# Four value loads moved from SyncE's DMA queue to ScalarE's in a retention-plus-FFN kernel

## The chip, the cores and the metric

The kernel runs on one core of a Trainium2 chip. The metric is the device time of one execution in microseconds, as the median of several runs. A "span" is the length of one profiled execution; it is about 2 us shorter than the time of the same run (196.0 against 198.11 us for the kernel before).

## The reference

Four sequences of 768 tokens with 8 heads of width 64 go through a decaying linear attention; the result, 3072 tokens of width 512, goes through a multiplicative FFN:

```python
# attention, per batch and head
state = gamma * state + outer(k[t], v[t])
y[t] = scale * (q[t] @ state)
# FFN on x = y of all heads side by side
out = ((x @ w1) * (x @ w2)) @ w3 @ w_out
```

All inputs and the output are float32. The kernel computes in fp16 with float32 accumulation, 24 chunks of 128 tokens.

## The kernel before

It first folds W3 and W_out into one matrix (TensorE transposes blocks of W3 and multiplies them with W_out), and the first chunks' attention is threaded into the end of that. All loads are issued by SyncE, in this order, at the very start of the program text:

```python
for i in range(4):
    w3c_st.append(load_w3_columns(i))
    wo_st.append(load_wo(i))
w3_st = {f: load_rows(moe_w3, f) for f in range(4, 8)}
load_chunk(0)                       # q of chunks 0 and 1, k and v of chunk 0
load_chunk(1)                       # k and v of chunk 1
w1_st = [load_rows(moe_w1, d) for d in range(4)]
w2_st = [load_rows(moe_w2, d) for d in range(4)]
for n in range(2, 6):
    load_chunk(n)
```

Each of these is 256 KB (k, v) or 512 KB (everything else). Nothing on SyncE has to wait for arithmetic here except W1 and W2, which reuse staging buffers.

The stretch into which the change reaches (cuts marked). `cast_w3` is a ScalarE cast of a W3 block to fp16, `w3_transpose` its transpose on TensorE, `w3_mm` the product with W_out with a copy of the result on ScalarE; `casts` is GpSimd's cast of q and k and its product of v with the decay factors:

```python
cast_w3(4, w3_st[4])
cast_w3(5, w3_st[5])
w3_mm_columns(3, acc)     # its last result is copied by ScalarE
w3_transpose(4)
w3_transpose(5)
cast_w3(6, w3_st[6])
w3_mm(4)
w3_transpose(6)
cast_w3(7, w3_st[7])
casts(0)
casts(1)
w3_mm(5)
# ... transposes, scores and kv of chunks 0 and 1, w3_mm(6), w3_mm(7) ...
cast_w(W1, w1_st, 1, False)
cast_w(W1, w1_st, 2, False)
cast_w(W1, w1_st, 3, True)      # True: on VectorE
cast_w(W2, w2_st, 0, True)
cast_w(W2, w2_st, 1, True)
```

Each engine has its own list of instructions, and the framework that builds the program adds the semaphores, counters that an instruction can wait for. In this program all hardware-queue transfers share eight completion semaphores, DMAHW0 to DMAHW7. (What is said here of the semaphores' names was read in the built programs. The traces don't name them; they show when an issue starts and when a transfer lands.)

## Time and profile before

| | |
|---|---|
| time | 198.95 us (198.35 to 199.02, 3 runs); 198.99 with a fourth run beside the changed kernel |
| span | 196.0 us |
| TensorE busy | 185.4 us, 95% |
| ScalarE busy | 97.1 us, 50% |
| transfers | 40.15 MB, the 16 engines nearly always busy for the first 150 us |

The page gives busy times and the chain of work that ended last. A line of a timeline is: start in us, duration in us, engine (SPq and ACTq are the sequencers of SyncE and ScalarE issuing transfers), source line, operation, what is written and read, count; in brackets the idle time before it and what ended it. The lines themselves stand in the prediction below.

### The profile page before, as it was taken

The numbers are of one execution on the slowest core, as the hardware profiler recorded it, in microseconds if no ns is written. First come the engines' busy times: TensorE is split into PE (matmuls) and PEld (weight loads), VectorE is DVE, ScalarE is ACT, GpSimd is POOL, SyncE is SP. The second block draws the span as 40 slices with busy tenths as digits, with TensorE's granted clock in tenths as the row PEclk, the third lists the DMA queues.
The fourth block names the chain that finished last, engine by engine and source line by source line (L and its number), as shares of the span: only waits on it lengthen the run. The fifth ranks groups of instructions, "written<-read, shape, count | busy, mean of one in ns | idle before, by whom it ended". The sixth has DMA issues, their size and how long they took to land.

```text
span 196.0 us, 4658 instructions
## 1 busy us (share of the span) xinstructions
PE 185.4 (95%) x1773; PEld 139.9 (71%) x1773; DVE 114.7 (59%) x215; ACT 97.1 (50%) x188; POOL 79.6 (41%) x137
## 2 busy tenths in 40 slices
PE   6798996999997999999999999999999999999992
PEld 2334665757995879778877887788778877887750
DVE  3226368757875767558555676575657665753310
ACT  6378547425443544546445454554455545534331
POOL 7200351166959636484423543854236432200000
PEclk9999999999999999999999999999999999999999
DMA  6999999989999999999999999979999630111112
GB/s 204 372 388 387 221 329 412 327 181 247 292 200 244 177 236 225 211 227 214 192 185 234 153 220 194 240 200 193 201 242 198 150 96 17 59 54 54 54 48 116
DMA packets 87446, 40.15 MB, mean 205 GB/s; under 512 B 67968, under 2 KB 82304, under 8 KB 87424
## 3 DMA queue, kind: packets, MB, share of 16 engines
q1 hardware_dynamic: 87424, 39.86, 91.0%
q8 instruction: 14, 0.23, 0.6%
q14 instruction: 8, 0.07, 0.2%
HBM read 29.36 MB, written 6.29 MB: 182 GB/s over the span
## 4 chain that ended last, share of the span: by engine, by line
PE 84%; DMA 6%; SPq 2%; DVE 2%; ACT 2%; POOL 1%; issue 1%; ACTq 0%; DVEq 0%; POOLq 0%
PE psF L427 39%; PE psO L453 21%; DMA stg<-in_moe_w_dram 6%; PE psA L361 5%; PE psW L254 4%; PE psY L399 3%; PE psY L400 3%; SPq L62 2%; PE psF L601 2%; PE psY L402 2%; PE psK L382 2%; PE psT L348 1%; PE psW L229 1%; DVE xt L407 1%; PE psYf L601 1%
## 5 line engine op out<-in xcount | busy, mean ns | idle before, releaser
L427 PE MATMUL psF<-xt,w 128*128 128x256 f16 (+1 forms) x768 | 87.1, 264 | 0.0
L427 PEld LDWEIGHTS <-w 128*128 128x128 f16 x768 | 68.1, 98 | 6.7
L437 ACT COPY pa<-psF 128x256 f32<-128x256 f32 x88 | 32.6, 372 | 35.7 <-PE psF L427 35.2
L443 DVE TENSOR_TENSOR ht<-pa,psF 128x256 f16<-128x256 f32 x88 | 36.7, 417 | 22.7 <-PE psF L427 10.6
L453 PE MATMUL psO<-w3o,ht 128*128 128x512 f16 x192 | 45.4, 379 | 0.2 <-DVE ht L620 0.2
L364 DVE TENSOR_TENSOR am<-psA,keep 128x512 f16<-128x512 f32 x48 | 30.9, 685 | 23.8 <-PE psA L361 23.8
L391 POOL TENSOR_TENSOR t<-s,GS 128x512 f16<-128x512 f32 x16 | 20.7, 1296 | 47.1 <-DVE s L390 38.7
L280 POOL TENSOR_TENSOR vp<-v,VS 128x256 f16<-128x256 f32 x48 | 28.5, 615 | 11.7 <-PE psY L402 5.7
L453 PEld LDWEIGHTS <-ht 128*128 128x128 f16 x192 | 18.5, 98 | 18.4 <-DVE ht L620 1.0
L458 ACT ACTIVATE osb<-psO 128x512 f32<-128x512 f32 x24 | 14.3, 597 | 34.2 <-PE psO L453 34.2
L270 POOL CAST q<-q 128x1024 f16<-128x1024 f32 x12 | 12.4, 1037 | 22.3 <-DMA q<-in_q_dram 22.1
L407 DVE TENSOR_TENSOR xt<-psY,YS 128x512 f16<-128x512 f32 x24 | 17.7, 736 | 5.4 <-PE psY L402 4.3
L276 POOL CAST k<-k 128x512 f16<-128x512 f32 x24 | 14.7, 611 | 7.7 <-PE psK L382 7.0
L399 PE MATMUL psY<-am,vp 128*128 128x128 f16 x96 | 16.7, 219 | 1.0 <-DVE am L364 0.9
L400 PE MATMUL psY<-am,vp 128*128 128x128 f16 x96 | 16.7, 219 | 0.0
L361 PEld LDWEIGHTS <-kp 128*128 128x128 f16 x192 | 12.6, 98 | 5.4 <-ACT kp L194 0.7
L390 DVE TENSOR_TENSOR s<-psK,t 128x512 f32<-128x512 f32 x16 | 11.0, 690 | 3.3 <-PE psK L382 3.0
L212 DVE COPY w3t<-psW 128x1024 f16<-128x1024 f16 x8 | 5.5, 690 | 11.9 <-PE psW L220 8.6
L342 ACT COPY kp<-kT 64x512 f16<-64x512 f16 x16 | 9.9, 618 | 1.9 <-DMA kT<-k 1.5
L400 PEld LDWEIGHTS <-vp 128*128 128x128 f16 x96 | 9.4, 98 | 1.5 <-issue 1.2
L194 ACT CAST w3h<-stg 128x1024 f16<-128x1024 f32 x8 | 8.3, 1044 | 4.1 <-DMA stg<-in_moe_w_dram 4.1
L402 PE MATMUL psY<-qTd,t 128*128 128x128 f16 x56 | 10.1, 219 | 0.0
(66 smaller groups left out, 170.6 us busy)
## 6 DMA issues: line engine op xcount, KB each, us to landing
stg<-in_moe_w_dram SPq DMA_DIRECT2D x16, 512.0 KB, 8.1
q<-in_q_dram SPq DMA_DIRECT2D x12, 512.0 KB, 5.0
k<-in_k_dram SPq DMA_DIRECT2D x24, 256.0 KB, 5.4
v<-in_v_dram SPq DMA_DIRECT2D x24, 256.0 KB, 5.3
out_dram<-osb SPq DMA_DIRECT2D x24, 256.0 KB, 2.4
stg<-in_moe_w_out_dram SPq DMA_DIRECT2D x4, 512.0 KB, 8.2
kT<-k SPq DMA_TRANSPOSE x16, 4.5
qTd<-q SPq DMA_TRANSPOSE x8, 4.3
```

What stands on the lines that cost most here:

```text
L276: nc.gpsimd.tensor_copy(k16[:, :], k32[:, :])
L280: nc.gpsimd.tensor_tensor(vp[:, :, r, r * 64 : r * 64 + 64], v32[:, :].rearrange("j (p s e) -> j p s e", s=2, e=64)[:, :, r, :], VS[:, :]. ...
L361: nc.tensor.matmul(ps[:, i, r, :], lhsT=kp[:, p, r, :], rhs=queries(n, p), start=True, stop=True)
L364: nc.vector.tensor_tensor(am[:, half * 2 : half * 2 + 2, :, :].rearrange("j p s i -> j (p s) i"), ps[:, :, :, :].rearrange("j p s i -> j ( ...
L391: nc.gpsimd.tensor_tensor(t16[:, :, :], s32[:, :, :], GS[:, :, :], MULT)
L399: nc.tensor.matmul(ps[:, p, :], lhsT=vp[:, p, 0, :], rhs=am[:, p, 0, :], start=True, stop=False)
L400: nc.tensor.matmul(ps[:, p, :], lhsT=vp[:, p, 1, :], rhs=am[:, p, 1, :], start=False, stop=(c == 0))
L407: nc.vector.tensor_tensor(XT[n // 2][:, :, n % 2 * C : (n % 2 + 1) * C].rearrange("p a (i t) -> p a t i", t=2), ps[:, :, :].rearrange(orde ...
L427: nc.tensor.matmul(ps[:, i * w : (i + 1) * w], lhsT=W[d][:, (f + i) * 128 : (f + i + 1) * 128], rhs=XT[self.tok0 // TB][:, d, c0 : c0 + w] ...
L437: nc.scalar.copy(self.pa[f][:, :], ps[:, :])
L443: nc.vector.tensor_tensor(self.HT[:, f : f + TB // self.width, :].rearrange("p f n -> p (f n)"), self.pa.pop(f)[:, :], ps[:, :], MULT,)
L453: nc.tensor.matmul(psO[:, :], lhsT=self.HT[:, f, tb * 128 : (tb + 1) * 128], rhs=W3O[f][:, :], start=(f == 0), stop=(f == 7),)
```

## The change

The intent: only q and k of the first chunks are urgent for TensorE's transposes; the values come later. If v of chunks 0 to 3 goes through ScalarE's own queue, issued when it is about to be needed, then W1, W2 and the next q and k move up in SyncE's queue.

```diff
+    def load_v(n):
+        chunk_in[n].append(load_kv(nc.scalar, "v", v, n))
 ...
         for nm, src in (("k", k), ("v", v)):
-            t = ld.tile([128, 512], FP, tag=nm + "32", name=nm + "32")
-            dma_in(...)
-            tiles.append(t)
+            if nm == "v" and n < 4:
+                continue
+            tiles.append(load_kv(nc.sync, nm, src, n))
 ...
     cast_w3(4, w3_st[4])
     cast_w3(5, w3_st[5])
+    load_v(0)
+    load_v(1)
     w3_mm_columns(3, acc)
 ...
     cast_w(W1, w1_st, 2, False)
+    load_v(2)
+    load_v(3)
     cast_w(W1, w1_st, 3, True)
```

(`load_kv` is the old body of the loop with the issuing engine as a parameter; cuts are marked with "...".)

More of the change, by code (lines that the diff above doesn't have):

```diff
@@ L65, with load_kv @@
     q_in = {}
+    def load_kv(eng, nm, src, n):
+        b, c = divmod(n, NCH)
+        t = ld.tile([128, 512], FP, tag=nm + "32", name=nm + "32")
+        eng.dma_start(
+            t[:, :].rearrange("p (h d) -> p h d", d=D),
+            src[b, :, c * C : (c + 1) * C, :].rearrange("h i d -> i h d"),
+        )
+        return t
+    def load_v(n):
+        chunk_in[n].append(load_kv(nc.scalar, "v", v, n))
     def load_chunk(n):
@@ L80, in load_chunk @@
         for nm, src in (("k", k), ("v", v)):
-            t = ld.tile([128, 512], FP, tag=nm + "32", name=nm + "32")
-            dma_in(
-                t[:, :].rearrange("p (h d) -> p h d", d=D),
-                src[b, :, c * C : (c + 1) * C, :].rearrange("h i d -> i h d"),
-            )
-            tiles.append(t)
+            if nm == "v" and n < 4:
+                continue
+            tiles.append(load_kv(nc.sync, nm, src, n))
         chunk_in[n] = tiles
```

## The prediction

> **What bounds the kernel now.** I began with the page: where each engine is busy, and the chain that ended last.
>
> ```profile
> PE 185.4 (95%) x1773; PEld 139.9 (71%) x1773; DVE 114.7 (59%) x215; ACT 97.1 (50%) x188; POOL 79.6 (41%) x137
> ...
> PE 84%; DMA 6%; SPq 2%; DVE 2%; ACT 2%; POOL 1%; issue 1%; ACTq 0%; DVEq 0%; POOLq 0%
> ```
>
> TensorE is busy for 185.4 of 196.0 us and carries 84% of the chain, so at most 10.6 us can be won. Then the waits of TensorE over the whole span say who owns those 10.6 us (columns: who waited, for whom, us in total, times, longest):
>
> ```profile
> PE psW L220 <- ACT w3h L194: 1.7, 4, 0.5
> PE psZ L534 <- DVE vp L133: 1.5, 1, 1.5
> PE psY L402 <- POOL t L391: 1.0, 1, 1.0
> PE psY L399 <- DVE am L364: 0.9, 1, 0.9
> PE psF L601 <- DVE xt L407: 0.6, 1, 0.6
> ```
>
> Only the first (W3 weights arriving, before 18 us) and the third (GpSimd late, at 59 to 60 us) have a transfer behind them. The change can't touch the first: all W3 loads are issued ahead of any value load.
>
> Next, ScalarE and TensorE in order of time around the place where the new issues stand. ScalarE (start, duration, what):
>
> ```profile
> 17.85 1.05 ACT L194 CAST w3h<-stg 128x1024 f16<-128x1024 f32 x1 [0.25 <-DMA stg<-in_moe_w_dram]
> 18.80 0.58 ACT L194 CAST w3o<-psWy 128x512 f16<-128x512 f32 x1
> 19.28 1.05 ACT L194 CAST w3h<-stg 128x1024 f16<-128x1024 f32 x1
> ```
>
> TensorE:
>
> ```profile
> 18.95 0.62 PE L229 MATMUL psW<-ident,w3h 128*128 128x128 f16 x8 [0.17 <-ACT w3h L194]
> 19.62 1.90 PE L254 MATMUL psW<-wo,w3t 128*128 128x512 f16 x8
> 21.36 0.61 PE L229 MATMUL psW<-ident,w3h 128*128 128x128 f16 x8
> 21.80 1.89 PE L254 MATMUL psW<-wo,w3t 128*128 128x512 f16 x8
> ```
>
> The ScalarE cast of 19.28 makes the fp16 rows of W3 block 6, which TensorE transposes at 21.36. It ends at 20.33, one microsecond early. In the windows view TensorE is busy for 10.00 of the 10 us from 20 to 30: what delays ScalarE by more than 1 us here delays the whole kernel.
>
> Last, the loads. SyncE's issues in order of time, and how long the issue of chunk 2's queries (at 28.26 us) took to land:
>
> ```profile
> 16.44 3.68 SPq L62 DMA_DIRECT2D v<-in_v_dram  x1
> 20.16 1.61 SPq L62 DMA_DIRECT2D k<-in_k_dram  x1
> 21.82 1.17 SPq L62 DMA_DIRECT2D v<-in_v_dram  x1
> 23.11 5.10 SPq L62 DMA_DIRECT2D stg<-in_moe_w_dram  x8
> 28.26 0.45 SPq L62 DMA_DIRECT2D q<-in_q_dram  x1
> ```
> ```profile
> DMA to landing us min/median/max: 11.9/11.9/11.9
> ```
>
> Adding the landing delay of each issue to its start gives a stream in strict order without a hole: k0 23.25, v0 24.6, k1 25.8, v1 26.8, the first W1 block 28.1, the last W2 block 37.0, chunk 2's q 40.1 (28.26 + 11.9), chunk 2's k 41.2. The transfer engines are the limit until about 50 us.
>
> **What the Trainium skill says.** "DMA: Bandwidth & Descriptors", section "Issuing engines are not separate DMA queues": transfers from different issuers run on the same 16 engines and interleave, and a second issuer saves only sequencer time. The trace of before has one issuing queue, so it can't show this; I take it as no gain in bandwidth. The same page, "Anatomy of one DMA": a transfer's semaphore wait is done by the issuing sequencer before dispatch. The trace agrees: chunk 2's q is issued at 28.26, just after the first W1 block has landed at 28.1, and the built program has it waiting for exactly that. "Perfetto Trace Analysis", section "DMA Instruction — HWDGE (DVE, Sync)": after that wait the sequencer locks the descriptor generator; not tested by one queue. "TensorE: Matmul & The Clock Gate", Part 1: after an idle window of about 3.4 us the array runs at half rate until it has been busy for such a window. The trace agrees: the first eight 128x512 matmuls take 3.60 us (450 ns each), five more from 6.42 us take 1.24 (248 ns).
>
> **The change part by part.** It takes four 256 KB loads off SyncE's stream and puts them on ScalarE: v0 and v1 after the cast of 17.85, v2 and v3 after the cast of W1 block 2.
>
> *The hidden part is a semaphore.* In the built programs every transfer takes the next of eight semaphores in program order and first waits until that semaphore's previous user has landed. The program text still issues the loads of chunks 2 to 5 at the top, before v0. In the changed program:
>
> ```
> SP   q, chunks 2 and 3  waits DMAHW7 >= 32, adds 16    (third user of DMAHW7)
> SP   k, chunk 2         waits DMAHW0 >= 48, adds 16
> ACT  v, chunk 0         waits DMAHW7 >= 48
> ACT  v, chunk 1         waits DMAHW0 >= 64
> ```
>
> So v0 can't be issued before chunk 2's q has landed, nor v1 before chunk 2's k. ScalarE meets these at about 19 us, and executes in order: behind them stand the copy of 18.80 and the cast of 19.28 that TensorE needs.
>
> *When does it go on?* Removing v0 and v1 from the stream advances all behind them by their own time, (24.6 - 23.25) + (26.8 - 25.8) = 2.35 us. So q of chunk 2 lands at 40.1 - 2.35 = 37.75 and k of chunk 2 at 38.85. v0 is issued from 37.75. An issue of k or v beside a full queue cost SyncE 1.0 to 4.3 us, and 1.0 at the least; ScalarE's own queue is empty, but the generator may be held by SyncE. I allow 1.7 us from k's landing to the end of the second issue (an estimate: 0.7 to issue, 1.0 for SyncE's turn): 40.6. Then the w3o copy holds ScalarE for 0.48 (18.80 to 19.28), the cast takes 1.05, and a handover 0.1: TensorE transposes at 42.2 instead of 21.36. **Delay: 20.9 us**, all of it on the path.
>
> *Cold restart.* TensorE has then idled for 20 us. At the start of before it took from 1.53 to about 6.4 us to reach full rate, some 4.4 us of them busy; half of that is lost: **+2.2 us**.
>
> *What comes back.* After the stall all first loads have landed. The wait of 1.0 us at 59 to 60 goes back to GpSimd's cast of chunk 6's q, which waited 1.44 us for its transfer behind a backlog; that backlog is gone: **-1.0 us**. W1 and W2 2.35 us earlier are worth nothing, as ScalarE is stopped.
>
> *v2 and v3.* Their semaphores are those of chunk 3's k and chunk 4's q, long landed by then. ScalarE idles 3.05 us just behind them (32.96 to 36.01 in before), so two issues of about 1 us cost nothing. Landing of v0: about 5 us after issue (4.6 to 5.7 in before beside a full queue), at about 43.5; its product is needed by the matmuls that stood at 26.82, now at about 48. Hidden.
>
> Sum: 198.95 + 20.9 + 2.2 - 1.0 = 221.05; I say **221**.
>
> **Rivals.**
> (a) *Only issue time.* If ScalarE didn't stop at the semaphore (or the wait were met at 19 us), two issues of 1.0 to 3.9 us (seen on SyncE) would stand before the cast, of which 1.0 is slack: +1 to +6 us, 200 to 205. Against it: the values 48 and 64 can't be reached before those loads land, which the trace puts near 40 us.
> (b) *The intended gain.* W1, W2, and the later q and k come 2.35 us earlier; with the only transfer-bound wait of TensorE after 20 us being 1.0, the gain would be at most 1 us: 198, within 2%. For it: the stream really is the bound of the loads until 50 us. Against: the semaphore again, and that TensorE waits for nothing of it.
> (c) *A longer stop.* The descriptor generator is shared, SyncE's issues hold it for 1 to 4 us each, and v0's packets alternate with those of chunk 2's k, so that k lands later and both issues take longer: up to 4 us more, 225. If v0 then landed later than 48 us, kv of chunk 0 would wait as well.
>
> **Range and chances.** The two landing times come from a stream in order and are good to about 1 us; the issues through a contended generator are uncertain by -1 to +3, the cold restart by 1 each way, the part that comes back by 1. I take 217 to 225 as the range. Rivals (a) and (b) need the wait to be absent from hardware though it stands in the program: 3% together, of which 2% within 2% and 1% faster.
>
> **What would show it.** ScalarE's timeline: a hole of about 20 us from 19 us on, ended by a transfer, with the two value issues on its queue near 38 and 39 to 40 us. TensorE: idle from about 21.4 to 42 before a transpose of W3, its releaser the w3h cast. Landing of chunk 2's q near 37.75. The first matmuls after the hole at about twice their duration start to start. From 60 us (before) on, the same distances shifted by a constant 21 to 23 us. The prediction is wrong if ScalarE works on through 20 to 38 us, if q of chunk 2 lands much earlier than 37 (a shorter stall), or if the issues on ScalarE take many microseconds each.

## The result

218.88 us (217.63 to 219.49, 4 runs) against 198.99 us (198.35 to 199.60, 4 runs). The ratio is 1.099 (95% interval 1.093 to 1.105). A ratio here is the mean time of one kernel's runs over that of the other's runs of the same rounds, so it isn't quite the ratio of the medians quoted.

The page of the changed kernel: TensorE's busy time hardly changed, its share fell. The rows of digits are tenths of busy time in 40 slices of 5.44 us; PEclk is the TensorE clock that was granted.

```profile
PE 186.8 (86%) x1773; PEld 140.3 (64%) x1773; DVE 115.7 (53%) x215; ACT 97.1 (45%) x188; POOL 80.5 (37%) x137
...
PE   6788000497799999999999999999999999999993
...
ACT  6473000537407454455554455564455464453332
...
PEclk9999755589999999999999999999999999999999
```

TensorE and ScalarE both stand still in three slices (22 to 38 us), and the granted clock is 0.7 in the first of them, then 0.5 until about 45.4 us, and full after that (0.52 from 43.5 to 45.4 us, 1.00 from 45.4 to 49). The work is the same; it is done later.

ScalarE in order of time, where the new issues stand (the lines that answer to those of 17.85, 18.80 and 19.28 us in the kernel before):

```profile
17.70 1.05 ACT L203 CAST w3h<-stg 128x1024 f16<-128x1024 f32 x1 [0.23 <-DMA stg<-in_moe_w_dram]
38.22 1.46 ACTq L70 DMA_DIRECT2D v<-in_v_dram  x2
39.72 0.58 ACT L203 CAST w3o<-psWy 128x512 f16<-128x512 f32 x1 [20.98 <-DMA k<-in_k_dram]
40.20 1.05 ACT L203 CAST w3h<-stg 128x1024 f16<-128x1024 f32 x1
```

It is the hole that was predicted: 20.98 us, ended by the landing of a **k**, though what stands in the queue are loads of **v**. Which k, and which q before it? Chunk 2's, issued by SyncE at 27.2 and 28.0 us. The next fence has what the trace says of these two issues (duration in ns, first and last start, then the time from issue to landing):

```profile
L62 SPq DMA_DIRECT2D q<-in_q_dram x1: 705/705/705, 27.2 to 27.2; - x1
DMA to landing us min/median/max: 11.0/11.0/11.0
L70 SPq DMA_DIRECT2D k<-in_k_dram x1: 666/666/666, 28.0 to 28.0; - x1
DMA to landing us min/median/max: 11.3/11.3/11.3
```

27.2 + 11.0 = 38.2: v0 is issued at 38.22. 28.0 + 11.3 = 39.3: v1 is issued at 39.30. Neither value load needs anything of chunk 2; they share its semaphores.

TensorE in order of time, against the lines of 19.62, 21.36 and 21.80 us of before:

```profile
19.47 1.90 PE L263 MATMUL psW<-wo,w3t 128*128 128x512 f16 x8
41.30 1.04 PE L238 MATMUL psW<-ident,w3h 128*128 128x128 f16 x8 [19.93 <-ACT w3h L203]
42.13 3.47 PE L263 MATMUL psW<-wo,w3t 128*128 128x512 f16 x8
45.43 0.61 PE L238 MATMUL psW<-ident,w3h 128*128 128x128 f16 x8
```

The transpose of W3 block 6 waits for its cast until 41.30 us, and the eight transposes and eight matmuls take 45.43 - 41.30 = 4.13 us where they took 23.53 - 21.36 = 2.17 us.

With start times of the same work on TensorE in both traces, the loss can be followed as it grows:

| TensorE starts | before | after | later by |
|---|---|---|---|
| transpose of W3 block 6 | 21.36 | 41.30 | 19.94 |
| transpose of W3 block 7 | 23.53 | 45.43 | 21.90 |
| first product with W1 | 32.92 | 54.82 | 21.90 |
| first output product (psO) | 40.76 | 63.50 | 22.74 |
| scores of chunk 3 | 47.43 | 70.17 | 22.74 |
| a later output product (psO) | 61.38 | 82.92 | 21.54 |
| end of the span | 196.0 | 217.6 | 21.6 |

So: +19.94 stop, +1.96 slow restart, +0.84 of something else at about 59 us, -1.20 given back at about 81 us, and nothing after that. The profiled run was the slowest of the four, and the profiled run of before was faster than its median; the medians differ by 19.9 us. So the hundredths hold for this pair of profiles alone. The stop itself varies from run to run: in e4 and e6 below, which issue the same loads in the same order, TensorE's transpose started at 40.59 and 40.41 us instead of 41.30.

The +0.84 was not in the prediction. TensorE's waits over the whole changed span show it as a new line, the second here:

```profile
PE psW L238 <- ACT w3h L203: 20.1, 2, 19.9
...
PE psF L614 <- DVE stg L201: 0.8, 1, 0.8
```

VectorE is late with copying W1's first product out of PSUM, because its three casts of weights ahead of that took 3.80 us instead of 2.97. GpSimd was at work beside them (VectorE's line in the kernel before, then VectorE's and GpSimd's in the changed one):

```profile
33.35 2.97 DVE L192 CAST w<-stg 128x1024 f16<-128x1024 f32 x3
...
55.25 3.80 DVE L201 CAST w<-stg 128x1024 f16<-128x1024 f32 x3
...
57.01 1.50 POOL L279 CAST q<-q 128x1024 f16<-128x1024 f32 x1
58.45 1.07 POOL L285 CAST k<-k 128x512 f16<-128x512 f32 x1
```

The same two GpSimd casts take 1.04 and 0.61 us in the kernel before, where they ran later, when q of chunk 2 had just landed. After the stop all data are there, so GpSimd starts at once, beside VectorE's casts. "SBUF — State Buffer", section "Who interferes with whom", of the Trainium skill says that VectorE in some modes and GpSimd take a shared port pair as an exclusive lock, and the later one blocks. Both being slow at once agrees with it. The experiment e6 below tests whether they slow each other; that this port is the reason is tested by no run.

### The profile page after: what moved, and what is told of

It is laid out like the page before. It is cut to its first block, busy times and chain, and to the rows that moved or that the text cites. A ratio compares the mean times of both kernels' runs of the same rounds, so it can differ in the third digit from the quotient of the medians.

```text
span 217.6 us, 4658 instructions
## 1 busy us (share of the span) xinstructions
PE 186.8 (86%) x1773; PEld 140.3 (64%) x1773; DVE 115.7 (53%) x215; ACT 97.1 (45%) x188; POOL 80.5 (37%) x137
## 4 chain that ended last, share of the span: by engine, by line
PE 74%; DMA 9%; SPq 8%; DVE 3%; issue 2%; ACT 1%; ACTq 0%; DVEq 0%
PE psF L436 35%; PE psO L462 19%; DMA k<-in_k_dram 5%; PE psA L370 5%; SPq L62 5%; DMA stg<-in_moe_w_out_dram 4%; SPq L70 4%; PE psW L263 3%; PE psY L408 2%; PE psY L409 2%; PE psY L411 2%; PE psK L391 2%; DVE w L201 1%; PE psF L614 1%; PE psTq L311 1%
## 5 line engine op out<-in xcount | busy, mean ns | idle before, releaser
L462 PE MATMUL psO<-w3o,ht 128*128 128x512 f16 x192 | 45.4, 379 | 0.2 <-DVE ht L633 0.2
L238 PE MATMUL psW<-ident,w3h 128*128 128x128 f16 x32 | 2.9, 242 | 20.1 <-ACT w3h L203 20.1
L279 POOL CAST q<-q 128x1024 f16<-128x1024 f32 x12 | 12.9, 1074 | 16.5 <-DMA q<-in_q_dram 16.5
L285 POOL CAST k<-k 128x512 f16<-128x512 f32 x24 | 15.6, 649 | 7.3 <-PE psK L391 7.2
L238 PEld LDWEIGHTS <-w3h 128*128 128x128 f16 x32 | 2.3, 111 | 21.4 <-ACT w3h L203 20.8
```

Source lines behind the costliest of these rows:

```text
L285: nc.gpsimd.tensor_copy(k16[:, :], k32[:, :])
L462: nc.tensor.matmul(psO[:, :], lhsT=self.HT[:, f, tb * 128 : (tb + 1) * 128], rhs=W3O[f][:, :], start=(f == 0), stop=(f == 7),)
```

## The experiments

Theory: ScalarE stands at the semaphore that v0 (then v1) reuses, until an unrelated transfer has landed; TensorE needs ScalarE's next cast; everything else follows. Rivals: issuing from ScalarE, or a second queue, is what costs; or the values themselves come too late. All eight kernels gave correct results. They ran on one chip, beside 7 or 8 runs of the kernel before: median 198.69 us for the first four (e1, e3, e4 and e5), 198.78 us for the others. The eight are the same seven and one more, so the later kernels are compared mostly with runs of the first batch. The changed kernel itself was timed in another session, so its 218.88 us is compared with these to about 1 us.

### e1_no_wait: the same issues, v0 and v1 on semaphores that are free

The loads of chunks 2 to 5 are written behind the last value load. (A small dictionary keeps the value tiles until then; the order of SyncE's loads and of ScalarE's instructions is unchanged.)

```diff
     w2_st = [load_rows(moe_w2, d) for d in range(4)]
-    for n in range(2, 6):
-        load_chunk(n)
 ...
     load_v(2)
     load_v(3)
+    for n in range(2, 6):
+        load_chunk(n)
```

> The changed kernel with the loads of chunks 2 to 5 written after the four value loads; SyncE's and ScalarE's orders of instructions stay as they are, apart from where the value loads take their semaphores. In the built program v0 and v1 now reuse semaphores of W3 column loads that land before 15 us, v2 one of a W1 block, v3 that of the first W2 block. Theory (ScalarE stands at a reused semaphore): no stop at 19 us, v0 and v1 issued near 17.8 us in about 0.4 us each, time 199.3 us (197.8 to 201.0); a small loss is possible because v2 and v3 then share the engines with the last W2 blocks. Rival (issuing from ScalarE, or a second queue, is itself costly): the time stays above 205 us.

Measured: 198.20 us (197.96 to 199.02), ratio 0.9985 (0.9941 to 1.0028): the whole loss is gone. ScalarE's timeline of this run:

```profile
17.27 1.05 ACT L201 CAST w3h<-stg 128x1024 f16<-128x1024 f32 x1 [0.23 <-DMA stg<-in_moe_w_dram]
17.29 1.06 ACTq L70 DMA_DIRECT2D v<-in_v_dram  x2
18.39 0.59 ACT L201 CAST w3o<-psWy 128x512 f16<-128x512 f32 x1
18.88 1.05 ACT L201 CAST w3h<-stg 128x1024 f16<-128x1024 f32 x1
```

Both issues are made within 1.06 us, while the cast of 17.27 runs. The next cast starts 1.12 us after it, where it took 0.95 us in the kernel before: 0.17 us, less than the 1.0 us that ScalarE has to spare there. Issuing from ScalarE and using a second queue cost nothing that can be seen in the time. There is no gain either: TensorE's wait of 1.0 us for GpSimd near 60 us is gone, but waits for GpSimd's casts of k have come, of 1.33 us the longest, at 43.86 us:

```profile
PE psT L356 <- POOL k L284: 1.6, 2, 1.3
```

The built program also corrected one detail. I had read the semaphores as dealt out in the order of the text. In this build v0 and v1, though written long after W1 and W2, stand ahead of them in the list of transfers and take semaphores of W3 columns that landed before 15 us. v2 and v3 did still wait in this run, on the semaphores that the expectation names: they are issued at 31.07 and 33.62 us, when W1 block 2 (31.1) and the first W2 block (33.6) land. It cost nothing, since ScalarE had its casts before them and nothing to do after them until 36.01. What counts is the order in which the build lists the transfers. In all builds a value load stands behind the value loads written before it; in the changed kernel those of chunks 4 and 5 were written first, so v0 stands behind all of chunks 2 to 5. Why the builder lists them so was not tested.

### e3_v23_only: only the second pair on ScalarE

```diff
-            if nm == "v" and n < 4:
+            if nm == "v" and n in (2, 3):
 ...
-    load_v(0)
-    load_v(1)
```

> Only v2 and v3 are loaded through ScalarE, v0 and v1 through SyncE as before. In the built program v2 waits for chunk 2's q, v3 for chunk 2's k, which landed at 40.1 and 41.2 us in the kernel before; ScalarE gets there at about 33 us. Theory: ScalarE stops for about 8 us, its copies of 36.0 us start at about 41.8, TensorE stands for some 5.5 us and restarts cold (1 to 2 us): 205.5 us (203 to 208.5). Rival (the stop belongs to the place of v0 and v1 alone, v2 and v3 are harmless as they were in the changed kernel): 198 to 200 us.

Measured: 203.94 us (203.68 to 204.76), ratio 1.027. In the changed kernel v2 and v3 were harmless only because the first stop had let everything land. Alone they stop ScalarE as well, at the copies that empty PSUM (the first two lines are ScalarE's timeline, the last is from TensorE's waits):

```profile
40.06 1.47 ACTq L70 DMA_DIRECT2D v<-in_v_dram  x2
41.63 1.07 ACT L203 COPY stg<-psF 128x512 f32<-128x512 f32 x2 [8.95 <-DMA k<-in_k_dram]
...
PE psF L612 <- ACT stg L203: 4.9, 1, 4.9
```

The expected start of those copies was 41.8, it is 41.63. The time is 1.6 us below the figure given, within its range: I hadn't taken off the 1.2 us that come back near 60 us. (In the traces TensorE's first output product is late by 47.73 - 40.76 = 6.97 us, the end by 201.8 - 196.0 = 5.8.)

### e5_v01_only: only the first pair on ScalarE

```diff
-            if nm == "v" and n < 4:
+            if nm == "v" and n < 2:
 ...
-    load_v(2)
-    load_v(3)
```

> Only v0 and v1 are loaded through ScalarE, v2 and v3 through SyncE. In the built program v0 then waits for v2 and v1 for chunk 3's k, one transfer each later than in the changed kernel. Theory: these land about 2.2 us later than chunk 2's q and k, at 40.4 and 41.5 us, and the whole kernel takes 2.2 us longer than the changed one: 221 us (219.5 to 222.5), though less of the work is on ScalarE's queue. Rival (the cost goes with the number of loads on ScalarE): less than the changed kernel, about 210 us.

Measured: 220.97 us (220.37 to 221.15), ratio 1.112, so about 2.1 us above the changed kernel with half as many loads on ScalarE. The semaphores that v0 and v1 get are now those of v of chunk 2 and k of chunk 3. The hole in ScalarE's timeline has grown from 20.98 to:

```profile
40.71 0.59 ACT L203 CAST w3o<-psWy 128x512 f16<-128x512 f32 x1 [22.63 <-DMA k<-in_k_dram]
```

Which transfer holds the semaphore sets the length of the stop, and moving fewer loads made it longer. The traces bear out the pairing issue by issue. In us, a value's issue and the landing of the transfer whose semaphore it reuses: v0 38.22 and 38.2, v1 39.30 and 39.3 in the changed kernel; v2 40.06 and 40.1, v3 41.16 and 41.1 in e3; v0 39.22 and 39.2, v1 40.29 and 40.3 in e5.

### e4_keep_warm: TensorE kept busy during the stop

```diff
     w3_mm(4)
+    busy(85)          # 85 matmuls of zeros, 128x512, results unused
     w3_transpose(6)
```

> The changed kernel with 85 idle matmuls (zeros, 128x512, results unused) put on TensorE ahead of the transpose that waits, so that it works through most of the stop. Theory: the transpose still starts at 41.3 us, but at full rate; the first transpose and the eight matmuls behind it take 2.2 us as in the kernel before instead of 4.1, and the time falls by 1.9 us to 217.0 us (216.0 to 218.0). Rival (the slow restart comes from something else, or is hidden later): no change, 218.9 us.

Measured: 216.61 us (216.29 to 216.73), 2.3 us below the changed kernel's median. In TensorE's timeline the stretch that took 4.13 us takes 42.78 - 40.59 = 2.19 us:

```profile
40.59 0.62 PE L238 MATMUL psW<-ident,w3h 128*128 128x128 f16 x8 [0.74 <-ACT w3h L203]
41.05 1.89 PE L263 MATMUL psW<-wo,w3t 128*128 128x512 f16 x8
42.78 0.61 PE L238 MATMUL psW<-ident,w3h 128*128 128x128 f16 x8
```

So the 1.96 us of the table are the restart at half rate, a cost of the idle time itself. The times alone wouldn't give that number: in this profile the stop also ended 0.71 us earlier (40.59 instead of 41.30).

### e6_casts_in_hole: VectorE's weight casts moved into the stop

```diff
     w3_mm(4)
+    cast_w(W1, w1_st, 3, True)
+    cast_w(W2, w2_st, 0, True)
+    cast_w(W2, w2_st, 1, True)
     w3_transpose(6)
 ...
-    cast_w(W1, w1_st, 3, True)
-    cast_w(W2, w2_st, 0, True)
-    cast_w(W2, w2_st, 1, True)
```

> The changed kernel with VectorE's three casts of W1 block 3 and W2 blocks 0 and 1 moved into the stop, ahead of the W3 transpose that waits, so that they no longer run beside GpSimd's casts of chunk 2. Theory (the 0.8 us that TensorE lost at 59 us in the changed kernel came from VectorE and GpSimd slowing each other): that wait vanishes, GpSimd's casts of q and k there take 1.04 and 0.61 us again instead of 1.50 and 1.07, the time falls by 0.8 us or a little more, to 218.0 us (216.8 to 218.6). Rival (GpSimd is slow there for another reason): its casts stay at 1.5 and 1.07 us.

Measured: 217.56 us (217.02 to 219.02, 6 runs), 1.3 us below the changed kernel's median, which by times alone isn't clear of the spread. The trace is clear: TensorE's wait for VectorE's copy is gone, VectorE's casts take 0.69 us each, and GpSimd's are fast again:

```profile
55.95 1.04 POOL L279 CAST q<-q 128x1024 f16<-128x1024 f32 x1
56.92 0.61 POOL L285 CAST k<-k 128x512 f16<-128x512 f32 x1
```

The +0.84 us was VectorE and GpSimd in each other's way. More than half of the 1.6 us between the two profiled spans (217.6 and 216.0) is something else: the stop ended 0.89 us earlier in this run.

### e7_sync_late: the same places in the text, issued by SyncE

```diff
-        chunk_in[n].append(load_kv(nc.scalar, "v", v, n))
+        chunk_in[n].append(load_kv(nc.sync, "v", v, n))
```

> The four value loads written at the same places as in the changed kernel, but issued by SyncE, so behind chunk 5's loads. Theory (what costs is ScalarE standing still): ScalarE works on past 19 us and the transpose at 21.3 us isn't late; but v0 lands only near 47 us, so TensorE stops later, at the first matmuls that use chunk 0's values (26.8 us), until about 48.7 us: a stop of 22 us in another place and with another releaser (GpSimd's product), 221 us (217 to 225). Rival (the stop of the changed kernel came from v0 being late, not from ScalarE): the stop stays at 21.3 us.

Measured: 221.64 us (220.37 to 222.29), ratio 1.115. The time is much the same as that of the changed kernel, but for another reason: ScalarE works on past 19 us, and TensorE stops later, at the first product with chunk 0's values. From ScalarE's timeline and TensorE's waits:

```profile
17.98 0.58 ACT L203 CAST w3o<-psWy 128x512 f16<-128x512 f32 x1
18.45 1.05 ACT L203 CAST w3h<-stg 128x1024 f16<-128x1024 f32 x1
...
PE psK L391 <- POOL vp L289: 21.8, 1, 21.8
```

So two things are apart here. In the changed kernel it is ScalarE that stops TensorE; v0 came in time after the stop (it landed at about 43.3 us, its product was done at 44.7, its first matmul at 48.73). In e7 it is v0, which lands near 47 us behind eight other loads. Equal times didn't mean an equal cause. It also follows (argued, not run) that letting ScalarE work on would not have been enough in the changed kernel: with v0 landing only at 43.3 us, TensorE would have stopped a little later, at that product.

### e8_chunk6_first: the part that came back, won without the change

The changed kernel gave back 1.2 us near 81 us. There TensorE in the kernel before waits for GpSimd, and GpSimd for chunk 6's q. This is the kernel before with one line moved:

```diff
+    load_chunk(6)
     f0.o_unit(0, chunk2_inputs)     # ends with an output store
 ...
-    load_chunk(6)
     t_new = kv(2)
```

> The kernel before, with chunk 6's loads issued ahead of the first two output stores instead of behind them; nothing on ScalarE's queue. Theory (TensorE's wait of 1.0 us at 60 us, which vanished in the changed kernel, comes from chunk 6's q landing late): q lands about 1.5 us earlier, the wait shrinks or vanishes, 198.0 us (197.3 to 198.8) against 198.7 to 199.0 before. Rival (the wait has another cause, or another takes its place): 198.9 us and TensorE's wait for t of 1.0 us stays.

Measured: 196.89 us (196.25 to 197.46, 6 runs) against 198.78 us, ratio 0.992 (0.988 to 0.996): faster, as the interval excludes 1, but by less than 2%. TensorE no longer waits for t. GpSimd casts chunk 6's q at 53.68 us instead of 55.33, and t is made at 57.05 instead of 58.82 (the first line is the kernel before):

```profile
55.33 1.04 POOL L270 CAST q<-q 128x1024 f16<-128x1024 f32 x1 [1.44 <-DMA q<-in_q_dram]
...
53.68 1.04 POOL L270 CAST q<-q 128x1024 f16<-128x1024 f32 x1 [0.23 <-DMA q<-in_q_dram]
...
57.05 1.28 POOL L391 TENSOR_TENSOR t<-s,GS 128x512 f16<-128x512 f32 x1
```

On TensorE the distance from chunk 6's query transposes to the next key transposes falls from 60.71 - 58.38 = 2.33 us to 59.06 - 57.94 = 1.12 us. The other 0.4 us of the difference of the two spans at this point are there already before these transposes; they were not traced to a cause.

### e9_both: v0 and v1 on ScalarE without a wait, and chunk 6 first

```diff
-            if nm == "v" and n < 4:
+            if nm == "v" and n < 2:
 ...                                  # loads of chunks 2 to 5 written after load_v(1),
+    load_chunk(6)                    # v2 and v3 stay on SyncE
     f0.o_unit(0, chunk2_inputs)
```

> Values of chunks 0 and 1 through ScalarE with no semaphore that is still in use, those of chunks 2 and 3 through SyncE, and chunk 6's loads ahead of the first output stores. Theory: v0 and v1 cost nothing on ScalarE and gain nothing, as the 16 engines are the limit; the gain is that of chunk 6 alone: 198.0 us (197.2 to 199.0). Rival (a second queue gets the first loads in sooner and TensorE gains from it): below 197 us.

Measured: 197.02 us (196.62 to 198.89, 6 runs), ratio 0.993 (0.988 to 0.998), the same as e8. Done rightly, the change's own idea brings nothing here; e8, with one moved line and one queue, is the version to keep.

## Why the prediction was right, and where its sizes were off

- **The mechanism** was right: ScalarE stood for 20.98 us at two reused semaphores, and was let go by chunk 2's q and k. e1 takes that away and the loss is gone (and with it the late landing of v0; e7 tells the two apart); e3 and e5 follow the same rule to 1.6 us or better of the figures given. v2 and v3 were harmless in the changed kernel, as said.
- **The landing times** 37.75 and 38.85 were 38.2 and 39.3. Chunk 2's q moved up by 40.1 - 38.2 = 1.9 us instead of 2.35, in this pair of profiles. In e4 and e6, with the same loads, v0 was issued at 37.42 and 37.28, so this miss is within what varies from run to run.
- **The issue term** was mis-sized: 1.7 us from k's landing to the end of the second issue was really 0.4 us (39.3 to 39.68). The two issues took 0.43 and 0.37 us, with SyncE issuing at the same time. So ScalarE went on at 39.72, not 40.6, and the stop was 19.94 us, not 20.9. Rival (c), the longer stop, rested on the same assumption and fell with it: v0 landed 5.1 us after its issue, in time. (The 4.6 to 5.7 us given for such landings were a choice: two loads of v in the kernel before, those issued at 16.44 and 33.72, took 8.2 and 8.6.)
- **The cold restart** of 2.2 us was 1.96 us, shown by e4.
- **What comes back**, 1.0 us, was 1.20 us, at the place named; e8 confirms the cause in the kernel before.
- **Left out** was the 0.84 us of VectorE and GpSimd, which start together once all data have landed (e6). That it makes up for much of the other errors is luck: 19.94 + 1.96 + 0.84 - 1.20 = 21.54 in the profiled run, against 22.1 predicted. By the medians the loss was 19.9, so 2.2 us less than predicted, of which up to about 1.5 us is the choice of runs (21.4 us lie between the two profiled runs).
- **Rival (a)**, issue time alone, was refuted by e1 (0.17 us of ScalarE's time, nothing in the kernel's; its upper end was also short, as two issues of 3.9 us less 1.0 are 6.8 us and not 6), **rival (b)**, the intended gain, by e1 and e9 (no gain even without the stop).
- **"In program order"** for the semaphores was too simple; it is the order in which the build lists the transfers.

## What to carry to other kernels

A load issued from a compute engine's queue brings that queue the load's waits, and one of them may be for a transfer that has nothing to do with it, because completion semaphores are reused: look in the built program for what the new issue waits on, and when that lands, before counting what the move saves. Placing such issues ahead of the text of later loads took the whole stop away here. And where two kernels take the same time (the changed one and e7), compare who waits for whom before believing in one cause.

## What the Trainium skill lacked or had wrong

- "DMA: Bandwidth & Descriptors", section "Rules for kernel authors", says that spreading transfers over several issuing engines only saves issue time. Lacking: it can stop a compute engine. Issues from ScalarE that reused the semaphores of pending transfers held ScalarE for 20.98 us here, and on free semaphores cost it 0.17 us (e1). That the issuer does the waiting is stated (the prediction cites it); no page says that the reuse of completion semaphores makes a load wait for an unrelated one.
- "Perfetto Trace Analysis", section "DMA Instruction — HWDGE (DVE, Sync)", has the descriptor generator locked for exclusive use by one sequencer. ScalarE's two issues took 0.43 us from 38.22 and 0.37 us from 39.30, inside issues of SyncE that ran from 37.96 to 38.99 and from 39.03 to 40.25, and 0.37 us at 51.11 with SyncE idle: ScalarE hardly waited for a lock. Whether SyncE did, within its own issues, the trace doesn't show.
- "SBUF — State Buffer", section "Who interferes with whom", agrees in kind with what was seen, but gives no size for plain casts: three 128x1024 casts on VectorE took 3.80 us beside GpSimd's product t and its casts, 2.97 us beside the product alone (the kernel before), and 3 x 0.69 us with GpSimd idle (e6); GpSimd's two casts took 1.50 and 1.07 us instead of 1.04 and 0.61.
